# Attention with a gated feed-forward block: sums of a fast matrix product moved between VectorE and GpSimd, and a small attention product moved one block on

## The chip, the cores and the metric

The kernel runs on one core of a Trainium2 chip. A core has engines that run side by side, each through its own instructions in order: TensorE (PE in the profile, its weight loads PEld) multiplies matrices into PSUM; VectorE (DVE) and ScalarE (ACT) work elementwise on PSUM and SBUF; GpSimd (POOL) works elementwise on SBUF; SyncE (SP) issues most transfers. An instruction that needs another engine's result waits for a semaphore, and everything behind it on its engine waits too. The metric is the device time of one execution in microseconds; less is better.

## The reference

Inputs are q, k and v with 8 batches, 8 heads, 576 positions and 64 features, and three weight matrices. For each batch and head:

```python
q_s = softmax(q, axis=-1)          # over the 64 features
k_s = softmax(k, axis=2)           # over the 576 positions
kv  = einsum('bhsd,bhse->bhde', k_s, v)
x   = einsum('bhsd,bhde->bhse', q_s, kv)
# x as 4608 rows of 512 features
out = (gelu(x @ w_gate) * (x @ w_val)) @ w_out     # 512 -> 1536 -> 512
```

The result is 4608 rows of 512, in float32.

## The kernel before, in words

**Blocks.** The rows are done in nine blocks of 512. Block b below 8 has positions of batch b; block 8 gathers the 64 positions that each of the 8 batches has left over. The order is 0 to 6, 8, 7. While the feed-forward of a block runs, the attention for later blocks is prepared beside it: exp of q and k on ACT, q's normalisation (`norm_pair`: a sum and a reciprocal on DVE, two multiplies on POOL), a transpose of q by a transfer (`unit_td`, L385), casts of v to half precision on POOL (`cast_v`, L188), kv (`unit_kv4`, L342: 40 small matmuls, then a reciprocal and a multiply on DVE) and x (`unit_x4`, L429).

**The feed-forward from block 3 on.** The hidden features, 1536, are twelve tiles of 128, called ht 0 to 11. Some tiles are made plainly: `half` makes "7g" (gate of tile 7, 4 matmuls of 512 columns, then Gelu on ACT) and "7v" (value, then the product on DVE, L626). The others are made in pairs k and k+3 by a fast scheme for two by two matrices that needs seven products in place of eight (`pair_step`). It needs sums of x (`sum_x`, L592, four subtractions on POOL) and of the weights (`sum_wgv`, L586, on DVE). A pair has four steps, written k.1 to k.4. Step 1 does products 1 and 5 and copies on ACT (L659 and `snap`, L639), step 2 products 6 and 3 and an addition on DVE (L643), step 3 products 7 and 2, another addition (L643), the first `final` (L632, L633) and `upper` (Gelu on ACT, L647, then a multiply, L649, on POOL, but on DVE for pair 8), step 4 product 4 and the second `final`. Product 4 adds into the bank that step 3's addition reads, so it waits for that addition.

**The output product.** `out_strassen` multiplies ht by w_out in the same scheme, product 1 to 7 (L711) in the banks psa, psb and psc. It copies a bank (`snap`, L743), adds (L749) into yo, and stores. It needs four sums of h (`sum_h`, L575): 1 and 2 go to separate tiles; 3 is written over a part of ht; 4 into s4. Each handles two j of six at a time. For j of 0 and 3, and of 1 and 4, they are made early, during the steps (names s0 and s1): 1 and 2 on DVE, 3 and 4 on POOL. For j of 2 and 5, which come last, all four are made within `out_strassen` on DVE. Product 5 needs sum 1, product 6 sum 2, product 3 sum 4, product 7 sum 3.

**The order.** It is written out by hand, and each engine runs its instructions in the order in which the program issues them. For blocks 3 to 8 the strings THREE, FOUR and SIX list the steps; letters are hooks: "a" and "n" the two halves of `norm_pair` for the next block, "t" the transpose of its q, "l" loads, "s0" and "s1" sums of h. Functions are hung on hooks with `at(block, kind, name, ...)` and run by `ride`. Kind PR means a name of these strings or "e" (exp of q and k, in `out_strassen`); kind NS means a place within `out_strassen`: 1 to 4 after products 5, 6, 3 and 7. Weight sums hang on NS 1 to 3, v's casts on NS 2, x, kv and the sums of x on NS 4. There is one buffer for exp of k and one for v in half precision, so exp of k and casts of v for a later batch must follow kv of the one before.

**Banks.** PSUM has 8 banks in a free list, `ring`; a new tile takes the oldest free one and waits for that bank's last reader.

Of the kernel before, what the change touches and what calls it, by code (L numbers as in the profile page):

```python
# [18 lines left out]
def kernel(  # L19
# [12 lines left out]
    B, H, S, D = q.shape  # L32
# [16 lines left out]
    NO = NFI // 2  # L49
# [43 lines left out]
    def let_go(t):  # L93
        ring.append(held.pop(id(t))[1])
# [26 lines left out]
    for i, nm in enumerate("gv"):  # L121
        n = 3 * NO * P
# [4 lines left out]
    xs_b = [xs, ld_b["v"][0].rearrange("p h x -> p (h x)").bitcast(f16)[:, 0:2048].rearrange(  # L127
        "p (i c r) -> p i c r", i=4, c=2)]
# [271 lines left out]
    def get_xt(b):  # L400
        if (b, "xt") not in st:
            st[(b, "xt")] = att.tile([P, HP, MAIN], f16, name="xt", tag="xt")
        return st[(b, "xt")]
# [161 lines left out]
    def sum_h(j0, j1, which, eng="dve"):  # L565
        step = 1 if j1 - j0 == 2 else NO // 2
        js, ks = slice(j0, j1, step), slice(NO + j0, NO + j1, step)
        a11, a21 = ht[:, js, 0:256], ht[:, js, 256:512]
        a12, a22 = ht[:, ks, 0:256], ht[:, ks, 256:512]
        s1, s2 = sh[1][:, js], sh[2][:, js]  # L570
        for i in which:
            o, a, b, op = {1: (s1, a21, a22, ALU.add), 2: (s2, s1, a11, ALU.subtract),
                           3: (a21, a11, a21, ALU.subtract),
                           4: (s4[:, js], a12, s2, ALU.subtract)}[i]
            (nc.gpsimd if eng == "pool" else nc.vector).tensor_tensor(out=o, in0=a, in1=b, op=op)  # L575
# [12 lines left out]
    def sum_x(xt, xs=xs):  # L588
        b11, b12, b21, b22 = (xt[:, c:c + 2, r:r + 256] for c in (0, 2) for r in (0, 256))
        t = [xs[:, i] for i in range(4)]  # L590
        for o, a, b in ((t[0], b12, b11), (t[1], b22, t[0]), (t[2], b22, b12), (t[3], b21, t[1])):
            nc.gpsimd.tensor_tensor(out=o, in0=a, in1=b, op=ALU.subtract)  # L592

    def product_gv(i, ps, xt, k, first):
# [3 lines left out]
        for t, w, nm in ((0, wv_sb, "v"), (1, wg_sb, "g")):  # L598
            ss = ws[(nm, k // NO)]
            for c in range(2):  # L600
# [6 lines left out]

    THREE = ("a 6g l 6v n 0.1 9g 0.2 9v t 0.3 7g 0.4 s0 1.1 7v 1.2 10g 1.3 10v 1.4 s1 2.1 8g 2.2"  # L610
             " 8v 2.3 11g 2.4 11v")
    FOUR = ("a 7g l 7v n 0.1 6.1 0.2 6.2 t 0.3 6.3 10g 0.4 6.4 s0 1.1 10v 1.2 8g 1.3 8v 1.4 s1 2.1"
            " 11g 2.2 11v 2.3")
    SIX = ("0.1 6.1 0.2 6.2 0.3 6.3 0.4 1.1 6.4 s0 7.1 1.2 7.2 1.3 7.3 1.4 2.1 7.4 s1 8.1 2.2 8.2"
           " 2.3 8.3 2.4")
    steps = {b: (THREE if b == 3 else SIX if b >= B - 1 else FOUR).split() for b in range(3, B + 1)}
    live = {}

# [82 lines left out]
    def product(i, ps, first, ts=(0, 1), js=range(NO)):  # L701
        for j in js:
            for t in ts:
                c0, c1 = slice(t * P, (t + 1) * P), slice(256 + t * P, 256 + (t + 1) * P)
                a = {1: ht[:, j, c0], 2: ht[:, NO + j, c0], 3: s4[:, j, c0], 4: ht[:, NO + j, c1],
                     5: sh[1][:, j, c0], 6: sh[2][:, j, c0], 7: ht[:, j, c1]}[i]
                w = {1: wo_sb[:, j, 0:256], 2: wo_sb[:, NO + j, 0:256],
                     3: wo_sb[:, NO + j, 256:512]}.get(i)
                if w is None:
                    w = tw[{4: 4, 5: 1, 6: 2, 7: 3}[i]][:, j]  # L710
                nc.tensor.matmul(ps[t], a, w, start=(first and j == js[0] and (  # L711
                    t == ts[0] or ps[t].tensor is not ps[ts[0]].tensor)),
                                 stop=(j == js[-1]), skip_group_check=True)

    def get_x(b):
        return get_xt(b) if b < B else xtr

    def last_js(b):
        return (NO - 2 if b < 3 else NO // 2 - 1, NO)

    def out_strassen(b, last):
        yo = [yop.tile([P, 2, C], f32, name="yo", tag="yo") for _ in range(2)]
        c = (slice(0, 256), slice(256, 512))
        ps, tiles_ = {}, {}

        def get(nm):
            if last:
                tiles_[nm] = [big([P, 256], f32, "ps" + nm, True) for _ in range(2)]
                ps[nm] = [x for x in tiles_[nm]]
            else:  # L730
                tiles_[nm] = [big([P, 2, 256], f32, "ps" + nm, True)]
                ps[nm] = [tiles_[nm][0][:, t] for t in range(2)]

        def parts(nm):
            return [(0, ps[nm][0]), (1, ps[nm][1])] if last else [(slice(0, 2), tiles_[nm][0])]

        def snap(nm):
            sn = ffn.tile([P, 2, 256], f32, name="sn", tag="gl")
            for n, (t, src) in enumerate(parts(nm)):
                if n:  # L740
                    nc.scalar.activation(out=sn[:, t], in_=src, func=ACTF.Copy, scale=1.0 / _H_SCALE)
                else:
                    nc.vector.tensor_scalar(out=sn[:, t], in0=src, scalar1=1.0 / _H_SCALE,  # L743
                                            scalar2=None, op0=ALU.mult)
            return sn

        def add(nm, sn, half, col):
            for t, src in parts(nm):
                nc.vector.scalar_tensor_tensor(  # L749
                    out=yo[half][:, t, c[col]], in0=src, scalar=1.0 / _H_SCALE,  # L750
                    in1=sn[:, t], op0=ALU.mult, op1=ALU.add)

        js = (0, 1, 2, 3, 4, 5) if b < 3 else (0, 3, 1, 4, 2, 5)
        get("a")
        product(1, ps["a"], True, js=js[:4])
        if b > 3:
            pair_step(b, get_x(b), NO // 2 - 1 if b < B - 1 else NFI - NO // 2 - 1, 4)
        ride(b, PR, "e")
        get("b")
        if 3 < b < B - 1:  # L760
            product(2, ps["b"], True, js=js)
        product(1, ps["a"], False, js=js[4:])
        sum_h(*last_js(b), (1, 2))
        s1 = snap("a")
        if not 3 < b < B - 1:
            product(2, ps["b"], True, js=js)
        add("b", s1, 0, 0)
        for x in tiles_["b"]:
            let_go(x)
        sum_h(*last_js(b), (4,))  # L770
        get("c")
        product(5, ps["c"], True, js=js)
        sum_h(*last_js(b), (3,))
        s5 = snap("c")
        ride(b, NS, 1)
        product(6, ps["a"], False, js=js)
        s2 = snap("a")
        ride(b, NS, 2)
        product(3, ps["c"], False, js=js)
        add("c", s2, 0, 1)  # L780
        ride(b, NS, 3)
        for x in tiles_["c"]:
            let_go(x)
        store_rows(b, 0, yo[0])
        if last:
            finish_last(b, ps["a"], yo[1], s5)
            return
        product(7, ps["a"], False, js=js)
        add("a", s5, 1, 1)
        ride(b, NS, 4)  # L790
        if b == B:
            go_on(B - 1, get_x(B - 1), 1)
        product(4, ps["a"], False, js=js)
        nc.scalar.activation(out=yo[1][:, :, c[0]], in_=tiles_["a"][0], func=ACTF.Copy,
                             scale=1.0 / _H_SCALE)
        let_go(tiles_["a"][0])
        store_rows(b, 1, yo[1])
# [97 lines left out]
    FI, NS, PR = range(3)  # L895
    plan = {}

    def at(b, kind, i, *fns):
        plan.setdefault((b, kind, i), []).extend(fns)

    L = lambda f, *a: (lambda: f(*a))
# [46 lines left out]
    for b in range(3, B):  # L948
        n = b + 1
# [12 lines left out]
    for b in range(2, B - 1):  # L962
        n = b + 1
        at(b, NS, 4, L(unit_x4, n, ("act", "dve"), 0 if n == B - 1 else None))
        if n + 1 < B:
            at(b, NS, 4, L(unit_kv4, n + 1, True))
        if b == 2:
            at(b, NS, 4, L(sum_wgv, "v", 4), L(sum_wgv, "v", 3), one_ring)
        if b < 6:
            at(b, NS, 4, L(preload, ACTF.Gelu))  # L970
        at(b, NS, 4, L(lambda n: sum_x(get_x(n)), n if n < B - 1 else B))
    at(B, PR, "s0", L(lambda: sum_x(get_x(B - 1), xs_b[1])))
    for b in range(3, B + 1):
        for j in range(NO // 2 - 1):
            at(b, PR, f"s{j}", L(sum_h, j, NO, (1, 2)), L(sum_h, j, NO, (3, 4), "pool"))
    for b, i, what in ((3, 1, "g1 v1"), (3, 2, "g2 v2 g3 v3"), (3, 3, "g4 v4")):
        for x in what.split():
            at(b, NS, i, L(sum_wgv, x[0], int(x[1]), NO, 1))
# [6 lines left out]
    def ride(b, kind, i):  # L985
        for fn in plan.get((b, kind, i), []):
            fn()
# [63 lines left out]
```

## Time and profile before

The median of three runs is 302.79 us (302.77 to 302.89). The profiled execution took 302.76 us, and its span from the first to the last instruction is 300.9 us.

| what | value |
|---|---|
| busy, share of the span | PE 285.8 us (95%), DVE 224.8 (75%), ACT 187.9 (62%), POOL 172.0 (57%) |
| granted TensorE clock | 1.00 |
| block 3, from its first matmul to block 4's | 113.86 to 144.84 us |
| blocks 4, 5, 6 | 144.84 to 176.07, to 207.30, to 237.13 |
| block 8 | 237.13 to 268.16 |
| block 7 and the end | 268.16 to 300.90 |
| a sum of h | DVE 417 to 526 ns, POOL 1154 and 1376 |
| a sum of x on POOL | 1154 to 1239 ns |
| a norm multiply on POOL | 1290 ns |

A line of the timeline gives start, duration, engine, source line, operation, the tiles written and read, and in brackets how long the engine stood idle before it and who released it. A line of the waits gives the total, the number and the longest. DMA engines are busy 56% of block 3 and 6% of block 8.

### The profile page before, as it was taken

Reading aid. Unit: us, or ns where it says so; the run is one execution under the profiler, and the core shown is the slowest. Engines: PE = TensorE matmul, PEld = TensorE weight load, DVE = VectorE, ACT = ScalarE, POOL = GpSimd, SP = SyncE. Lnnn points to the kernel's source line nnn. Section 1 sums busy time; section 2 is a strip of 40 time slices with the busy share of each in tenths; the row PEclk is TensorE's granted clock in tenths of the full one; section 3 lists DMA queues with packets and bytes.
Section 4 is the critical chain, followed back from the end, with each engine's and each line's share of the span. In section 5 each row is a group of like instructions: output and inputs, shape, how many; then the busy total and the mean of one; then the engine's idle time right before and its main releaser. Section 6 shows DMA issues by size and latency. Waiting matters only on the chain. (4 is left out here: it accounts for less than half of the span.)

```text
span 300.9 us, 6202 instructions
## 1 busy us (share of the span) xinstructions
PE 285.8 (95%) x2401; PEld 198.8 (66%) x2401; DVE 224.8 (75%) x430; ACT 187.9 (62%) x305; POOL 172.0 (57%) x157
## 2 busy tenths in 40 slices
PE   3999999999999999999999899989999998899994
PEld 1544445447744586668777777777768786788884
DVE  2943478998677889769876996889678586946792
ACT  4763467767652566676866877686861677338740
POOL 1557557870346009873896579757972579504720
PEclk9999999999999999999999999999999999999999
DMA  7999999996189106930697049603130300033003
GB/s 230 372 383 390 401 388 395 324 309 179 74 291 314 26 34 226 369 73 2 191 379 150 1 163 382 156 0 137 37 67 0 142 2 2 0 72 70 2 1 142
DMA packets 54622, 51.72 MB, mean 172 GB/s; under 512 B 18496, under 2 KB 50496, under 8 KB 54592
## 3 DMA queue, kind: packets, MB, share of 16 engines
q1 hardware_dynamic: 52864, 49.49, 51.9%
q10 hardware_dynamic: 1728, 1.84, 1.9%
q8 instruction: 19, 0.31, 0.4%
q14 instruction: 11, 0.09, 0.1%
HBM read 37.75 MB, written 9.44 MB: 157 GB/s over the span
## 5 line engine op out<-in xcount | busy, mean ns | idle before, releaser
L466 PE MATMUL psg<-xt,wg_sb 128*128 128x512 f16 x216 | 57.4, 379 | 0.0
L466 PE MATMUL psv<-xt,wv_sb 128*128 128x512 f16 x216 | 57.4, 379 | 0.0
L249 POOL TENSOR_TENSOR eq<-eq,rrq 128x640 f16<-128x640 f16 (+1 forms) x27 | 34.7, 1304 | 19.5 <-DVE rrq L242 7.2
L711 PEld LDWEIGHTS <-ht 128*128 128x128 f16 x384 | 37.2, 98 | 6.0 <-issue 0.8
L471 ACT ACTIVATE gl<-psg 128x512 f32<-128x512 f32 x36 | 21.0, 598 | 28.8 <-PE psg L466 28.6
L472 DVE SCALAR_TENSOR_TENSOR ht<-psv,gl 128x512 f16<-128x512 f32 x36 | 24.2, 684 | 16.0 <-PE psv L466 13.7
L466 PEld LDWEIGHTS <-wv_sb 128*128 128x128 f16 x216 | 21.1, 98 | 22.3 <-issue 0.2
L466 PEld LDWEIGHTS <-wg_sb 128*128 128x128 f16 x216 | 21.0, 98 | 20.7
L605 PEld LDWEIGHTS <-wv_sb 128*128 128x128 f16 x216 | 20.9, 98 | 11.3 <-issue 3.0
L649 POOL TENSOR_TENSOR ht<-eq 128x512 f16<-128x512 f32 x13 | 16.5, 1272 | 20.5 <-ACT eq L647 20.5
L188 POOL CAST v<-vt 128x640 f16<-128x640 f32 x26 | 20.2, 818 | 12.0 <-PE pskv L342 10.5
L592 POOL TENSOR_TENSOR xs<-xt 128x512 f16<-128x512 f16 x8 | 9.6, 1194 | 29.3 <-ACT xt L190 29.3
L711 PE MATMUL psa<-tw,ht 128*128 128x256 f16 x192 | 23.5, 273 | 0.1
L605 PEld LDWEIGHTS <-wg_sb 128*128 128x128 f16 x216 | 21.1, 98 | 2.5
L212 ACT ACTIVATE ek<-kt 128x1280 f16<-128x1280 f32 (+1 forms) x11 | 19.1, 1748 | 5.7 <-DMA kt<-in_k_dram 4.2
L659 ACT COPY pgb<-pga 128x512 f32<-128x512 f32 x27 | 15.9, 590 | 10.2 <-PE pga L605 10.0
L633 DVE SCALAR_TENSOR_TENSOR ht<-pga,glq 128x256 f16<-128x256 f32 x27 | 11.1, 422 | 13.7 <-ACT glq L632 13.7
L711 PEld LDWEIGHTS <-sh 128*128 128x128 f16 x192 | 18.8, 98 | 3.7 <-issue 1.6
L575 POOL TENSOR_TENSOR ht<-ht 128x512 f16<-128x512 f16 x12 | 16.5, 1376 | 6.3 <-DVE sh L575 6.3
L632 ACT ACTIVATE glq<-pgb 128x256 f32<-128x256 f32 x27 | 10.2, 378 | 15.8 <-PE pgb L605 9.5
L212 ACT ACTIVATE eq<-qt 128x2560 f16<-128x2560 f32 (+2 forms) x10 | 18.4, 1863 | 2.6 <-DMA qt<-in_q_dram 2.5
L605 PE MATMUL pga<-xs,wv_sb 128*128 128x256 f16 x84 | 16.0, 272 | 2.9 <-DVE eq L643 2.3
(161 smaller groups left out, 677.8 us busy)
## 6 DMA issues: line engine op xcount, KB each, us to landing
out_dram<-yo SPq DMA_DIRECT2D x15, 512.0 KB, 3.4
kt<-in_k_dram SPq DMA_DIRECT2D x7, 640.0 KB, 8.9
vt<-in_v_dram SPq DMA_DIRECT2D x7, 640.0 KB, 5.4
qt<-in_q_dram SPq DMA_DIRECT2D x7, 640.0 KB, 7.3
qt<-in_q_dram SPq DMA_DIRECT2D x8, 512.0 KB, 7.7
wost<-in_moe_w_out_dram SPq DMA_DIRECT2D x6, 512.0 KB, 7.9
kt<-in_k_dram SPq DMA_DIRECT2D x6, 512.0 KB, 9.7
vt<-in_v_dram SPq DMA_DIRECT2D x6, 512.0 KB, 6.0
```

The costliest lines, as they stand in the source:

```text
L188: nc.gpsimd.tensor_copy(out=dst, in_=src)
L212: nc.scalar.activation(out=dst[:, n0:NC, h0 * D:h1 * D].rearrange(o, d=D, **({"t": 2} if b >= QUAD else {})), in_=heads(tiles[(nm, b)], b, ...
L249: (nc.gpsimd if eng == "pool" else nc.vector).tensor_tensor(out=e, in0=e, in1=rrq.unsqueeze(-1).to_broadcast((P, n, 2, D)), op=ALU.mult)
L466: nc.tensor.matmul(ps, w[:, ci, fi * P:(fi + 1) * P], xt[:, ci, :], start=(ci == 0), stop=(ci == HP - 1))
L471: nc.scalar.activation(out=gl, in_=psg, func=ACTF.Gelu)
L472: nc.vector.scalar_tensor_tensor(out=ht[:, fi, :], in0=psv, scalar=_H_SCALE, in1=gl, op0=ALU.mult, op1=ALU.mult)
L575: (nc.gpsimd if eng == "pool" else nc.vector).tensor_tensor(out=o, in0=a, in1=b, op=op)
L605: nc.tensor.matmul(ps[:, t], a, x, start=(first and t == 0 and c == 0), stop=(c == 1), skip_group_check=True)
L633: nc.vector.scalar_tensor_tensor(out=ht[:, fi, 0:256], in0=ps[:, 0], scalar=_H_SCALE, in1=gl, op0=ALU.mult, op1=ALU.mult)
L649: (nc.vector if k == NFI - NO // 2 - 1 else nc.gpsimd).tensor_tensor(out=ht[:, k:k + NO // 2 + 1:NO // 2, 256:512], in0=cc[:, :, 0], in1=c ...
L659: nc.scalar.copy(out=pb, in_=pa)
L711: nc.tensor.matmul(ps[t], a, w, start=(first and j == js[0] and (t == ts[0] or ps[t].tensor is not ps[ts[0]].tensor)), stop=(j == js[-1]), ...
```

## The change

It changes the order of work and, for some sums, the engine; the arithmetic is the same.

- In `out_strassen`, sums 4 and 3 of the last j go to POOL for blocks above 2; both are issued ahead of v's casts at NS 2.
- A new place NS 0 lies after the first eight matmuls of product 1. kv of batches 5, 6 and 7 moves there, from NS 4 of blocks 3, 4, 5 to NS 0 of blocks 4, 5, 6. kv of batch 4 stays in block 2.
- Sums of x for block 7 move from s0 of block 8 to NS 4 of block 6, behind those for block 8.
- The hooks s0 and s1 keep sums 1 and 3; sums 2 and 4 go to new hooks u0 and u1. In the strings, sums stand later: in THREE both behind 7v, in FOUR behind 1.1, 1.2, 2.1 and 2.2, in SIX behind 7.1, 1.3, 8.1 and 2.3.
- In THREE, "n" moves behind 0.4, 1.1 ahead of 7v, and "t" behind 1.1.

```diff
-    THREE = ("a 6g l 6v n 0.1 9g 0.2 9v t 0.3 7g 0.4 s0 1.1 7v 1.2 10g 1.3 10v 1.4 s1 2.1 8g 2.2"
-             " 8v 2.3 11g 2.4 11v")
-    FOUR = ("a 7g l 7v n 0.1 6.1 0.2 6.2 t 0.3 6.3 10g 0.4 6.4 s0 1.1 10v 1.2 8g 1.3 8v 1.4 s1 2.1"
-            " 11g 2.2 11v 2.3")
-    SIX = ("0.1 6.1 0.2 6.2 0.3 6.3 0.4 1.1 6.4 s0 7.1 1.2 7.2 1.3 7.3 1.4 2.1 7.4 s1 8.1 2.2 8.2"
-           " 2.3 8.3 2.4")
+    THREE = ("a 6g l 6v 0.1 9g 0.2 9v 0.3 7g 0.4 n 1.1 t 7v s0 u0 1.2 10g 1.3 10v 1.4 s1 u1 2.1 8g"
+             " 2.2 8v 2.3 11g 2.4 11v")
+    FOUR = ("a 7g l 7v n 0.1 6.1 0.2 6.2 t 0.3 6.3 10g 0.4 6.4 1.1 s0 10v 1.2 u0 8g 1.3 8v 1.4 2.1"
+            " s1 11g 2.2 u1 11v 2.3")
+    SIX = ("0.1 6.1 0.2 6.2 0.3 6.3 0.4 1.1 6.4 7.1 s0 1.2 7.2 1.3 u0 7.3 1.4 2.1 7.4 8.1 s1 2.2"
+           " 8.2 2.3 u1 8.3 2.4")
...
         product(1, ps["a"], True, js=js[:4])
+        ride(b, NS, 0)
         if b > 3:
...
-        sum_h(*last_js(b), (4,))
+        sum_h(*last_js(b), (4,), "pool" if b > 2 else "dve")
         get("c")
         product(5, ps["c"], True, js=js)
-        sum_h(*last_js(b), (3,))
+        sum_h(*last_js(b), (3,), "pool" if b > 2 else "dve")
...
     for b in range(2, B - 1):
         n = b + 1
         at(b, NS, 4, L(unit_x4, n, ("act", "dve"), 0 if n == B - 1 else None))
-        if n + 1 < B:
+        if b == 2:
             at(b, NS, 4, L(unit_kv4, n + 1, True))
+        if b > 3:
+            at(b, NS, 0, L(unit_kv4, n, True))
...
-    at(B, PR, "s0", L(lambda: sum_x(get_x(B - 1), xs_b[1])))
+    at(6, NS, 4, L(lambda: sum_x(get_x(B - 1), xs_b[1])))
     for b in range(3, B + 1):
         for j in range(NO // 2 - 1):
-            at(b, PR, f"s{j}", L(sum_h, j, NO, (1, 2)), L(sum_h, j, NO, (3, 4), "pool"))
+            at(b, PR, f"s{j}", L(sum_h, j, NO, (1,)), L(sum_h, j, NO, (3,), "pool"))
+            at(b, PR, f"u{j}", L(sum_h, j, NO, (2,)), L(sum_h, j, NO, (4,), "pool"))
```

## The prediction

> **What bounds the kernel now.** I read the page first: busy shares, then the chain that ended last, then the waits of PE, then the timelines around each wait.
>
> ```profile
> PE 285.8 (95%) x2401; PEld 198.8 (66%) x2401; DVE 224.8 (75%) x430; ACT 187.9 (62%) x305; POOL 172.0 (57%) x157
> ...
> PE 11%; DVE 1%; issue 0%
> ```
>
> PE is busy 95% of the 300.9 us span and carries the chain, so an edit counts only where PE stands still. PE's waits from 113 us on, where all edits lie:
>
> ```profile
> PE pga L605 <- DVE eq L643: 2.3, 2, 1.2
> PE psc L711 <- DVE sn L743: 1.5, 3, 0.5
> PE psa L711 <- DVE sn L743: 1.2, 2, 0.6
> PE pga L605 <- DVE cc L643: 0.6, 1, 0.6
> ```
>
> All are PE waiting for DVE. PE's timeline places them (the wait in brackets):
>
> ```profile
> 121.58 0.39 PE L605 MATMUL pga<-xs,wv_sb 128*128 128x256 f16 x2 [0.62 <-DVE cc L643]
> ...
> 168.67 1.47 PE L711 MATMUL psa<-tw,sh 128*128 128x256 f16 x12 [0.61 <-DVE sn L743]
> 170.67 1.47 PE L711 MATMUL psc<-wo_sb,s 128*128 128x256 f16 x12 [0.52 <-DVE sn L743]
> ...
> 250.35 0.38 PE L605 MATMUL pga<-xs,wv_sb 128*128 128x256 f16 x2 [1.17 <-DVE eq L643]
> ```
>
> Recorded ends carry pipeline latency, so I measure gaps by starts (12 matmuls of 256 columns take 1.31, 4 of 512 take 0.87): block 3: 0.78; blocks 4 and 5: 0.77+0.69 each; block 6: 0.59; block 8: 1.34, 1.30, 0.30. Together 7.2 us, the most that can be won. Why DVE is late, from DVE's and POOL's timelines in block 8:
>
> ```profile
> 246.10 1.11 DVE L575 TENSOR_TENSOR sh<-ht 128x512 f16<-128x512 f16 x1
> 247.24 1.26 DVE L575 TENSOR_TENSOR sh<-sh,ht 128x512 f16<-128x512 f16 x1
> 248.43 0.68 DVE L643 SCALAR_TENSOR_TENSOR eq<-pgc,snq 128x512 f32<-128x512 f32 x1
> ...
> 245.78 1.15 POOL L592 TENSOR_TENSOR vt<-xt 128x512 f16<-128x512 f16 x1
> 247.00 1.22 POOL L592 TENSOR_TENSOR vt<-xt,vt 128x512 f16<-128x512 f16 x1
> ```
>
> A sum of h takes DVE 0.42 alone; here each ends 0.28 after a POOL instruction ends (246.93, 248.22). The sums at 166.26 and 167.20 lie so against v's casts (0.91, 0.82).
>
> **The skill.** The Trainium skill's "SBUF — State Buffer", section "Who interferes with whom", gives DVE and GpSimd one shared port pair with an exclusive lock; its section "SBUF: two separate sides" says the lock is held for a whole instruction and counts DVE instructions with two SBUF inputs. The lines above agree; additions with one PSUM input keep 0.68 beside POOL. "Perfetto Trace Analysis", section "GPSIMD Instruction", advises timing POOL by start-to-start spacing: I use 1.12 for a sum of h or x (recorded 1.15; 1.40 behind a DVE sum), 1.22 for a norm multiply, 1.23 for upper's multiply (L649), 0.66 for a cast of v.
>
> **The change, part by part.** Times are before's own, unless called new.
>
> *Block 3: norm's second half behind step 0.4, sums 1 and 2 of h together behind 7v.* Removed: DVE's reduce (1.47) and reciprocal no longer stand before the additions of step 0.3, so its addition ends at about 120.5, step 0.4 starts unhindered at 120.80 and 1.1 follows. Added: after 0.4's last DVE instruction (new 122.05 to 122.5) come the reduce to 123.9, the reciprocal to 124.2, and 7v's product to 124.75. POOL's two norm multiplies run from 124.2 to 126.7. Sum 1 wants to start at 124.7, waits for the first multiply (125.5) and ends at 125.78; sum 2 waits for the second and ends at 126.98. Behind them on DVE: the addition of 1.2 to 127.6 and that of 1.3 to 128.2. Step 1.4 overwrites what the latter reads and starts at 128.25, where 127.24 was before and 126.45 was free: **+1.0**, the 0.78 won included. Without the lock it would be 126.98, or -0.26.
>
> The transpose of eq (one DMA on SP) leaves at about 126.75 instead of 122.88. Landing 6.4 to 8.4 later, it is done by 135.2; the next exp of q, which overwrites eq, starts at 135.43 plus this shift, and SP's next job is the store at 141.75. Cost nothing; uncovered, ACT would slip, with 2.4 us of idle before 142.44.
>
> *kv one block on.* Its 40 matmuls (0.75 on PE) leave blocks 3, 4, 5 and enter 4, 5, 6: PE's work is unchanged. Exp of k now waits for kv, but stands behind a table load and the exp of q (3.6 us) on ACT: nothing. Kv's reciprocal and multiply (0.17+0.42) fall into DVE's 0.83 idle before step 2.4's product: nothing. Following the free list by hand, kv takes 8v's bank, long read. But kv had covered something: between x's matmuls and product 4, which overwrites psa after yo's addition has read it. That addition ends 0.9 after product 7; x's matmuls cover 0.7. Any lateness of DVE there now reaches PE.
>
> *Third and fourth sums of the last pair on POOL ahead of the casts.* DVE loses 2 times 0.33. Sums 1 and 2 no longer meet the casts: in block 4 they end at new 167.5 (upper on POOL being 0.3 later, since sum 2 of s1 moved), the copy of psa at 168.2, before product 6 wants it at 168.66. POOL makes sum 4 to 168.7 and sum 3 to 169.85; product 3 wants the fourth at 169.97, product 7 the third at 171.28. So 0.77+0.69 is won in blocks 4 and 5, and 0.59 in 6. But casts now run from 169.8 to 172.9, onto DVE's weight sums (L586, 0.42 each). In block 4: g1 ends 171.45, g2 172.3, yo's addition 172.9, g4 173.2, next yo's addition 173.86; product 4 starts at 173.9 instead of 174.75: **-0.85**. Block 5 (two sums, norm of the rest 0.9): 205.6 against 205.98: **-0.38**. Block 6 (no casts, kv added): 236.0 against 235.82: **+0.18**. Block 3: eight small sums among the casts, product 4 at 144.53 against 143.51: it keeps its **+1.0**.
>
> *Sums of x of block 7 with block 8's, and single sums, block 8.* POOL's eight sums run to 245.65, so upper of pairs 0 and 6 ends at 248.1 (245.8 before). Sum 1 waits for it, runs clear to 248.57; then additions, 1.3's to 250.36: step 1.4 at 250.41 against 250.35. That stall stays: the lock is exchanged for a queue. Sum 2 behind 1.3 pushes ACT's copies by 0.37, so 2.2 and 8.2 start 0.2 to 0.4 later. Upper of 7 ends at 254.7, sum 1 at 255.2, addition of 2.3 at 257.28: step 2.4 at 257.33 against 258.09. Call that addition's end A. POOL's upper of pair 2 ends at A+2.02, with its fourth sum queued behind it (u1 comes after 2.3). DVE's own upper of pair 8 (two SBUF inputs; alone about 0.69 by "VectorE: DVE Perf Modes", section "The TRN2 errata — SBUF-src ops pay a fixed extra latency per instruction") is ready at A+2.0. A tie. If POOL is first, DVE ends at A+3.7, the product of 8.4 and psb's last two matmuls wait, and product 3 starts at 264.24 against 264.50: **-0.26**. If DVE is first: 263.69, -0.81. In the first case the shorter copy chain behind psc also takes away the 0.30.
>
> *Single sums in blocks 4 to 6.* Sum 1 of s0 waits for upper as before (155.81); sum 2, now behind 1.2's addition, meets POOL's sum 3 and ends at new 157.71; 1.3's addition ends at 158.33 (158.49 before) and step 1.4 starts at 158.97. Of s1 it fills 0.3 of the idle time that was 0.76, and 2.3's addition ends at 164.5, before 2.4 at new 165.16, which kv pushed back. Nothing; without kv there, 0.1.
>
> *Block 7.* No wait of PE to win here. Sum 2 behind 1.3 and 2.3 moves additions and ACT's copies by 0.31 and PE with them. The same tie: POOL first, psb waits 0.8 more and product 3 starts at 294.12 against 293.02: **+1.1**; DVE first: +0.32.
>
> **Sum.** POOL first: 1.0-0.85-0.38+0.18-0.26+1.1 = +0.8. DVE first: 1.0-0.85-0.38+0.18-0.81+0.32 = -0.54. The profiled execution took 302.76, 1.86 outside its span, and the median is 302.79: 303.6, or 302.25. I take POOL first, because its instruction waits ready in the queue while DVE's still needs ACT's result.
>
> **Rivals.** (1) DVE gets the pair first, in both blocks: 302.25, not slower. It decides at A+2.0: a gelu 0.05 earlier suffices. For it: at 135.28 a DVE sum asking 0.1 before a cast ended was let in ahead of the next. Against: no such margin here. (2) Block 3's sums pass the norm multiplies: 1.25 us less, 302.3 with POOL first, 301.0 with DVE first. For it: multiplies of the norm starting 0.5 sooner or sums 2 us later would do. Against: all three starts hang on one reciprocal, and the DVE subtraction from 61.47 to 63.37 (1.9, the one before it 0.96) waited out just such a multiply, which ended at 62.55. (3) The simple reading: all named stalls go and nothing comes, 7.2 us less, 295.6. Against: 1.9 us of POOL queue in block 8 and the lost cover behind x. I give it next to nothing. (4) More goes late than I found, such as a slipped exp on ACT or casts meeting every weight sum: block 4 and 5 win nothing (+1.2 on the sum): 304.8.
>
> **Numbers.** POOL first 0.40, DVE first 0.26, block 3 clear 0.12, more late 0.20, all stalls gone 0.02. About 0.2% (0.6 us) is what can be told from no change. Faster (below 302.2): half of DVE first, most of block 3 clear: 0.22. Within: the other half, and the lower end of POOL first: 0.30. Slower (above 303.4): 0.48. Both signs hold most of the chance; POOL first alone spans 303.0 to 304.2. The range, 301.5 to 304.8, reaches from block 3 clear to more late.
>
> **What would show it.** Right: no wait at 168.67 and 170.67 and their likes; step 1.4 of block 3 waiting nearly 2 us for an addition, with two sums of h over 1 us on DVE; product 4 of blocks 3 to 5 waiting for yo; 1.4 of block 8 still waiting over 1 us; psb of block 7 waiting for ht behind a long L649 on DVE. Wrong: sums of 0.42 in block 3, POOL's eight sums of x not delaying upper, or L649 on DVE below 0.8 in blocks 8 and 7.

## The result, and the profile after

The changed kernel takes 302.95 us (median; 302.83 to 303.24) beside 302.78 us for the kernel before in the same session (302.76 to 302.89). The ratio is 1.0006, with a 95% interval of 0.9989 to 1.0023: no change that can be told. One run below was profiled in an execution of 309.05 us at a granted clock of 0.95, so of it only the time of its three other executions is used.

The page of the changed kernel, busy times and the chain that ended last:

```profile
PE 285.7 (95%) x2401; PEld 198.5 (66%) x2401; DVE 220.8 (73%) x418; ACT 188.2 (63%) x305; POOL 184.3 (61%) x169
...
PE 7%; ACT 2%; DVE 1%; issue 1%; ACTq 0%
```

DVE has lost 4.0 us of work and POOL has gained 12.3, as meant; PE's busy time and the span (301.0 against 300.9 us) have not moved. PE's waits from 113 us on, after the change (total, number, longest); yo is written by the additions of the output product, sn by the copies of its banks, and eq and cc at L643 by the additions of a pair:

```profile
PE pga L605 <- DVE eq L643: 3.2, 2, 1.8
PE psa L711 <- DVE yo L749: 2.2, 3, 0.9
PE pga L605 <- ACT pgb L659: 0.3, 2, 0.2
```

The 2.7 us for the copies sn are gone, and so is the wait for cc. In their place stand 2.2 us for yo and 0.9 more for eq. PE's timeline says where:

```profile
128.45 0.38 PE L605 MATMUL pga<-xs,wv_sb 128*128 128x256 f16 x2 [1.81 <-DVE eq L643]
144.83 1.47 PE L711 MATMUL psa<-tw,ht 128*128 128x256 f16 x12 [0.80 <-DVE yo L749]
175.24 1.47 PE L711 MATMUL psa<-tw,ht 128*128 128x256 f16 x12 [0.46 <-DVE yo L749]
206.10 1.47 PE L711 MATMUL psa<-tw,ht 128*128 128x256 f16 x12 [0.92 <-DVE yo L749]
250.91 0.38 PE L605 MATMUL pga<-xs,wv_sb 128*128 128x256 f16 x2 [1.35 <-DVE eq L643]
```

These are waits of the same kind, PE for DVE, and all but the last stand at new places: step 1.4 of block 3, product 4 of blocks 3, 4 and 5, step 1.4 of block 8. To see what each block won or lost, take one fixed point in each, the start of product 4 in blocks 3 to 6 and of product 3 in 8 and 7; "block" is the time from the point before to this one. The two runs at the right are described below.

| start of | before | after | block, before | block, after | only the last pair's sums moved | all but kv moved |
|---|---|---|---|---|---|---|
| block 2, product 4 | 112.54 | 112.57 | | | 112.65 (start) | 112.75 (start) |
| block 3, product 4 | 143.51 | 144.83 | 30.97 | 32.26 | 31.10 | 32.25 |
| block 4, product 4 | 174.75 | 175.24 | 31.24 | 30.41 | 29.76 | 29.99 |
| block 5, product 4 | 205.98 | 206.10 | 31.23 | 30.86 | 29.82 | 30.12 |
| block 6, product 4 | 235.82 | 236.21 | 29.84 | 30.11 | 29.25 | 29.46 |
| block 8, product 3 | 264.50 | 264.31 | 28.68 | 28.10 | 28.38 | 28.11 |
| block 7, product 3 | 293.02 | 293.16 | 28.52 | 28.85 | 28.52 | 28.85 |

So the change won 0.83 + 0.37 + 0.58 us in blocks 4, 5 and 8 and lost 1.29 + 0.27 + 0.33 in blocks 3, 6 and 7. In block 3, DVE's timeline shows the two sums that the prediction expected beside the norm's multiplies:

```profile
124.63 1.16 DVE L575 TENSOR_TENSOR sh<-ht 128x512 f16<-128x512 f16 x1
125.83 1.37 DVE L575 TENSOR_TENSOR sh<-sh,ht 128x512 f16<-128x512 f16 x1
```

They take 2.53 us where two of 0.42 would do. And the tie of block 8, first DVE's lines and then POOL's:

```profile
259.83 0.69 DVE L649 TENSOR_TENSOR ht<-cc 128x512 f16<-128x512 f32 x1
...
260.77 1.04 DVE L575 TENSOR_TENSOR sh<-ht 128x512 f16<-128x512 f16 x1
```

```profile
259.85 1.69 POOL L575 TENSOR_TENSOR s<-ht,sh 128x512 f16<-128x512 f16 x1
```

DVE's multiply started 0.02 us ahead of POOL's sum, took its clear 0.69, and POOL's sum of 1.15 recorded 1.69; DVE's next sum, beside it, took 1.04 in place of 0.42. Block 7 shows the same: DVE at 289.01, POOL at 289.03. That is the opposite of what the prediction chose.

### The profile page after: what moved, and what is told of

Its sections match the earlier page's. It is cut to its first block, busy times and chain, and to the rows that moved or that the text cites. A ratio compares the mean times of both kernels' runs of the same rounds, so it can differ in the third digit from the quotient of the medians.

```text
span 301.0 us, 6201 instructions
## 1 busy us (share of the span) xinstructions
PE 285.7 (95%) x2401; PEld 198.5 (66%) x2401; DVE 220.8 (73%) x418; ACT 188.2 (63%) x305; POOL 184.3 (61%) x169
## 5 line engine op out<-in xcount | busy, mean ns | idle before, releaser
L575 POOL TENSOR_TENSOR s<-ht,sh 128x512 f16<-128x512 f16 x18 | 21.9, 1215 | 10.8 <-DVE sh L575 10.8
L649 POOL TENSOR_TENSOR ht<-eq 128x512 f16<-128x512 f32 x13 | 16.5, 1272 | 17.0 <-ACT eq L647 17.0
L575 POOL TENSOR_TENSOR ht<-ht 128x512 f16<-128x512 f16 x18 | 21.2, 1179 | 6.1 <-DVE sh L575 6.1
```

The lines of the kernel that those rows point to most:

```text
L649: (nc.vector if k == NFI - NO // 2 - 1 else nc.gpsimd).tensor_tensor(out=ht[:, k:k + NO // 2 + 1:NO // 2, 256:512], in0=cc[:, :, 0], in1=c ...
```

## Experiments

The theory is that of the prediction: PE waits only where DVE is late, and DVE is late because its sums with two SBUF inputs wait while POOL works, or because POOL's queue brings their input late. What is open is which part of the change pays and which costs. The diffs show the orders and calls that differ, shortened. Unless said otherwise each run is the changed kernel with one edit. Times are medians; the kernel before took 302.78 to 302.92 in these sessions.

### Sums of block 3 behind step 1.3

```diff
-1.1 t 7v s0 u0 1.2 10g 1.3 10v 1.4
+1.1 t 7v 1.2 10g 1.3 s0 u0 10v 1.4
```

> The changed kernel with one edit: in block 3 both sums of h of the first pair stand behind step 1.3 in place of step 1.2, so the additions of 1.2 and 1.3 no longer queue behind them on DVE while POOL multiplies the norm. Theory (sums held up by POOL's norm multiplies through the shared port pair, additions queued behind them): step 1.4 of block 3 starts at about 126.5 in place of 128.45, nothing comes back later in the block, time 302.95 - 1.9 = 301.0 us. Rival (the wait is only the reduce and reciprocal of the norm on DVE, or the slack is eaten at 2.4 by sums that now meet sums 3 and 4 on POOL): 1.4 or 2.4 still waits over 1 us, time 302.5 to 303.0.

Measured: 301.95 us, 0.9969 of before (0.9957 to 0.9981). The wait at 1.4 is gone, but DVE's second sum of the first pair now meets POOL's multiply of upper, that of the next pair meets POOL's fourth sum, and step 2.4 waits. DVE's timeline, POOL's, then PE's:

```profile
127.19 1.38 DVE L575 TENSOR_TENSOR sh<-sh,ht 128x512 f16<-128x512 f16 x1
...
129.90 1.26 DVE L575 TENSOR_TENSOR sh<-sh,ht 128x512 f16<-128x512 f16 x1
```

```profile
126.97 1.31 POOL L649 TENSOR_TENSOR ht<-eq 128x512 f16<-128x512 f32 x1
...
129.54 1.33 POOL L575 TENSOR_TENSOR s<-ht,sh 128x512 f16<-128x512 f16 x1
```

```profile
133.00 0.38 PE L605 MATMUL pga<-xs,wv_sb 128*128 128x256 f16 x2 [0.60 <-DVE cc L643]
```

Step 1.4 had lost 1.97 us, measured by starts. Half of it is won (product 4 of block 3 comes 1.0 us sooner), half is given back one pair later: between the two expectations.

### The norm's multiplies behind the sums

```diff
-0.4 n 1.1 t 7v s0 u0 1.2
+0.4 n 1.1 7v s0 u0 m t 1.2      # n: reduce and reciprocal; m: the two multiplies on POOL
```

> The changed kernel with one edit: in block 3 the two POOL multiplies of the norm's second half, and the transpose issue, stand behind the sums of s0 and u0 in the order, the norm's reduce on DVE stays where it is. Theory (DVE's two sums of h take 1.16 and 1.37 us because POOL's multiplies work beside them): the sums take about 0.42 each, step 1.4's wait of 1.81 us falls to under 0.4. But POOL's product of the upper half of pair 1 now waits behind the multiplies until about 131, so the sums of s1 come late and step 2.4 waits some 1.5 us instead: 302.6 to 302.9. Rival (the reduce itself, 1.2 us of DVE ahead of the sums, is what is late): the sums take 0.4 but step 1.4 still waits over 1 us, and the time is 303.5 or more.

Measured: 303.14 us, 1.0010 (1.0002 to 1.0019). DVE's sums, then PE's next wait:

```profile
124.58 0.41 DVE L576 TENSOR_TENSOR sh<-ht 128x512 f16<-128x512 f16 x1
125.03 0.42 DVE L576 TENSOR_TENSOR sh<-sh,ht 128x512 f16<-128x512 f16 x1
```

```profile
134.03 0.38 PE L606 MATMUL pga<-xs,wv_sb 128*128 128x256 f16 x2 [1.51 <-DVE cc L644]
```

The reduce stands where it stood, at 122.33 and 1.48 long, and the sums take 0.41 and 0.42. So the 1.7 us of block 3 are the multiplies beside the sums, and the rival, the reduce, falls. The time is not won, because the upper product of pair 1 now queues behind the multiplies (it starts at 130.00), and step 2.4 waits 1.51, as expected. The total came 0.24 above the expected range.

### kv at its old place

```diff
-at(b, NS, 0, L(unit_kv4, n, True))       # b = 4, 5, 6
+at(b, NS, 4, L(unit_kv4, n + 1, True))   # b = 3, 4, 5
```

> The changed kernel with kv back at its old place, between x and product 4 (blocks 3, 4, 5), the rest as changed. Theory (kv covered the wait of product 4 for yo's addition; at its new place it covers nothing, so its 0.75 us on PE comes on top): block 3 ends as in the changed kernel, blocks 4 and 5 end 0.3 earlier each, block 6 loses the 0.75 and wins about 0.5; waits of PE for yo shrink to 0.2 or less; time about 301.9 us. Rival A (kv's place makes no difference, since PE's work is the same): 302.8 to 303.1. Rival B (all three waits for yo, 2.2 us, come from the move): 300.8.

Measured: 301.16 us, 0.9945 (0.9931 to 0.9960), faster than both kernels. All of PE's waits from 113 us on:

```profile
PE pga L605 <- DVE eq L643: 3.2, 2, 1.8
PE pga L605 <- ACT pgb L659: 0.3, 2, 0.2
```

No wait for yo is left. The ledger's last column differs from the changed kernel by 0.42, 0.74 and 0.65 us in blocks 4, 5 and 6: kv's move alone costs 1.8 us. Kv's 40 matmuls take 0.75 us wherever they stand; standing ahead of product 4 they fill time that PE would wait, and standing in product 1 they fill none. In block 3 product 4 starts at the same distance with kv and without (32.25 and 32.26); of three times 0.75 us, 1.81 is so filled. The expectation of 1.05 was too small.

### Sums of x of block 7 back in block 8

```diff
-at(6, NS, 4, L(lambda: sum_x(get_x(B - 1), xs_b[1])))
+at(B, PR, "s0", L(lambda: sum_x(get_x(B - 1), xs_b[1])))
```

> The changed kernel with the sums of x of block 7 back at the first sums of h of block 8, the rest as changed. Theory (the stall at step 1.4 of block 8 was only changed from a lock into a queue behind eight sums of x on POOL): POOL's two uppers end 2 us earlier, 1.4 waits less than 0.3 in place of 1.35, but POOL is late for pair 7 and step 2.4 waits about 1.3; block 8 is about 0.5 shorter, time 302.4 us. Rival (moving them was worth what it seems to be, a stall less): time 303.6 or more, with both stalls over 1 us.

Measured: 303.12 us, 1.0008 (0.9998 to 1.0018). DVE's second sum, and PE's waits of 0.5 us and more in block 8:

```profile
250.21 1.35 DVE L575 TENSOR_TENSOR sh<-sh,ht 128x512 f16<-128x512 f16 x1
```

```profile
252.22 0.38 PE L605 MATMUL pga<-xs,wv_sb 128*128 128x256 f16 x2 [0.73 <-DVE cc L643]
...
258.45 0.38 PE L605 MATMUL pga<-xs,wv_sb 128*128 128x256 f16 x2 [0.56 <-DVE eq L643]
```

One wait of 1.35 turns into one of 0.73 and one of 0.56. Beside the other parts, this part of the change is neutral: POOL's sums of x cost about as much ahead of its products as beside DVE's sums.

### The last pair's sums back on DVE

```diff
-sum_h(*last_js(b), (4,), "pool" if b > 2 else "dve")      # and so for (3,)
+sum_h(*last_js(b), (4,))
```

> The changed kernel with the last pair's third and fourth sums of h back on DVE in all blocks, the rest as changed. Theory (on POOL they keep the casts away from sums 1 and 2 and take 0.66 from DVE ahead of psc's copy, at the price of casts falling on the weight sums): waits of product 6 and product 3 come back in blocks 4, 5 and 6 at 0.3 to 0.6 each, block 3 wins 0.5 because its eight weight sums run clear, blocks 4 and 5 lose 0.7 each, blocks 6 and 8 lose 0.3 to 0.5; time about 304.5 us. Rival (the two ways of meeting POOL are worth the same): 302.8 to 303.2.

Measured: 305.22 us, 1.0081 (1.0064 to 1.0098), so undoing this part costs 2.3 us. Two of PE's waits in this run:

```profile
PE psc L711 <- DVE sn L743: 2.2, 5, 0.6
PE psa L711 <- DVE yo L749: 0.6, 3, 0.2
```

Psc waits for its copy again. But the wait for yo shrank from 2.2 us to 0.6, so an estimate of what these sums are worth by themselves is 2.3 + 1.6 = 3.9.

### The last pair's sums alone

The kernel before, with that one edit.

> The kernel before with one part of the change alone: the last pair's third and fourth sums of h on POOL, all else as before. Theory (the psc snapshot waits for DVE behind these sums; putting them back on DVE in the changed kernel cost 2.3 us, and kv at its old place covers the waits for yo): 300.7 to 301.3. Rival (without the other parts POOL has not finished its casts and upper products by then, and products 3 wait for the fourth sum): 302.5 to 303.5.

Measured: 299.17 us, 0.9879 (0.9864 to 0.9894): 3.7 us faster than before, 1.5 below the expected range, which had been read off the run above without the wait that it hid. PE's waits from 113 us on, then sums 1 and 2 of block 4 on DVE, before and in this run, and POOL in this run:

```profile
PE pga L605 <- DVE eq L643: 2.3, 2, 1.2
PE pga L605 <- DVE cc L643: 0.6, 1, 0.6
```

```profile
166.26 0.91 DVE L575 TENSOR_TENSOR sh<-ht 128x512 f16<-128x512 f16 x1 [0.37 <-POOL ht L649]
167.20 0.82 DVE L575 TENSOR_TENSOR sh<-sh,ht 128x512 f16<-128x512 f16 x1
```

```profile
166.47 0.43 DVE L575 TENSOR_TENSOR sh<-ht 128x512 f16<-128x512 f16 x1 [0.37 <-POOL ht L649]
166.93 0.42 DVE L575 TENSOR_TENSOR sh<-sh,ht 128x512 f16<-128x512 f16 x1
167.28 0.68 DVE L743 TENSOR_SCALAR sn<-psa 128x512 f32<-128x512 f32 x1
```

```profile
167.44 1.16 POOL L575 TENSOR_TENSOR s<-ht,sh 128x512 f16<-128x512 f16 x1 [1.00 <-DVE sh L575]
```

Sums 1 and 2 took 0.91 and 0.82 before, beside v's casts. POOL now has sum 4 queued ahead of the casts, and sum 4 needs sum 2, so POOL stands still while DVE makes its two: 0.43 and 0.42. The copy of psa stands right behind these two. The copy of psc stood behind sums 4 and 3 as well, two of 0.42 that are now gone from DVE. In block 6 no casts run and sums 1 and 2 took 0.43 and 0.42 before too, so there only the second effect is at work. Both waits of psc and psa for sn are gone, and with kv still in front of product 4 none for yo takes their place. By the ledger this one edit wins 1.48, 1.41, 0.59 and 0.30 us in blocks 4, 5, 6 and 8. All the rest of the change gives it back: 1.16 in block 3, 0.23, 0.30 and 0.21 in blocks 4 to 6 by the order of the sums, 1.81 by kv, 0.33 in block 7, less 0.28 in block 8.

### The norm's second half earlier (kv at its old place)

```diff
-a 6g l 6v 0.1 9g 0.2 9v 0.3 7g 0.4 n 1.1 t 7v s0 u0 1.2 10g 1.3 10v 1.4 s1 u1 2.1 8g 2.2 8v 2.3 11g 2.4 11v
+a 6g l 6v 0.1 9g 0.2 9v 0.3 n 7g 0.4 1.1 t 7v s0 1.2 10g 1.3 u0 10v 1.4 2.1 8g s1 2.2 8v 2.3 u1 11g 2.4 11v
```

> The changed kernel with kv at its old place (measured alone: 301.16) and block 3's order rewritten: norm's second half stands ahead of half 7g, where DVE shows about 1 us of idle time, and the sums u0 and s1 stand one step later each. Theory (the stall of 1.97 us at step 1.4 of block 3 comes from the norm beside the sums): it falls to under 0.5, and 299.6 to 300.0 comes out. Rival (the norm's reduce then delays the additions of steps 0.3 and 0.4, and the stall only moves to steps 1.1 to 1.3): 300.8 to 301.3.

Measured: 299.70 us, 0.9897 (0.9880 to 0.9913), as the theory had it. DVE's timeline:

```profile
121.03 1.48 DVE L240 TENSOR_REDUCE rq<-eq 128x20 f32<-128x1280 f16 x1
...
123.85 0.58 DVE L575 TENSOR_TENSOR sh<-ht 128x512 f16<-128x512 f16 x1
...
126.66 0.41 DVE L575 TENSOR_TENSOR sh<-sh,ht 128x512 f16<-128x512 f16 x1
...
128.24 1.36 DVE L575 TENSOR_TENSOR sh<-ht 128x512 f16<-128x512 f16 x1 [0.23 <-POOL ht L649]
```

The reduce moves 1.3 us forward, into time that DVE had idle, and the sums take 0.58 and 0.41. The first sum of the next pair now meets POOL (1.36), but PE does not wait for it: no wait in block 3 is over 0.2 us. Since sums moved too, the 1.46 us against the run with kv alone are those of the whole order.

### Sums of x of block 8 on DVE (kv at its old place)

```diff
+    if mid: mid()          # in unit_x4, behind the copies of xtr: sum_x(xtr) on DVE
```

> The changed kernel with kv at its old place (measured alone: 301.16) and the four sums of x of block 8 on DVE, straight behind the copies of xtr, those of block 7 alone on POOL. Theory (POOL is late in block 8 by the eight sums in a row, and step 1.4's gap of 1.51 us there is POOL's upper product coming late): that gap falls to under 0.4, 299.6 to 300.0. Rival (the sums, some 1.7 us of DVE at the end of block 6, delay DVE's copies of x and the PSUM banks behind them, and a wait of the same length comes at block 8's first steps): 300.9 to 301.5.

Measured: 300.73 us, 0.9931 (0.9915 to 0.9948): 0.4 us under the run with kv alone and 0.2 under the rival's range, far from the theory's. The first mix below, which holds this edit too, shows part of why: the wait of 1.35 at step 1.4 is gone, but one of 0.57 for ACT stands in the first steps of block 8, where the run with kv alone has none. What delays ACT there was not followed.

### Three mixes

All three have kv at its old place, the early norm, the order of before in blocks 4 to 6 and the edit just named. The first keeps the changed order in blocks 7 and 8, the second takes the order of before there (s0 and u0 together ahead of 7.1), the third sets them together behind 7.1.

> A version put together from the parts that paid: kv at its old place; the last pair's sums on POOL; block 3's order with the norm early (as in the run that measured 299.70); blocks 4 to 6 with the order of before, so that sums of h of one step stand together; blocks 7 and 8 with the order of the changed kernel; sums of x of block 8 on DVE behind the copies of xtr, those of block 7 on POOL ahead of block 8. From the start points of the runs so far: 299.70, less 0.75 for blocks 4 to 6, less 0.7 to 1.4 for block 8, so 297.5 to 298.3. Rival (DVE's sums of x at the end of block 6 only move the wait of block 8, as the 0.33 us gained by that run suggests): 298.6 to 299.2.

> As the mix before it in this call, with the order of before in blocks 7 and 8 too (the sums s0 and u0 ahead of step 7.1, s1 and u1 ahead of 8.1). Theory (the two gaps of 1.35 and 1.30 us that this order showed in block 8 come from POOL being late with its eight sums of x, not from where DVE's sums stand): both gaps under 0.4, and 297.0 to 298.0. Rival (the order itself: DVE's two sums wait at the head of its queue for POOL's upper product): one of the gaps stays at 0.7 us or more, 298.3 to 299.0.

> As the first mix of this call, with s0 and u0 together, and s1 and u1 together, behind steps 7.1 and 8.1 in blocks 7 and 8, where DVE showed about 1 us of idle time ahead of steps 1.2 and 2.2. Theory: the four sums fall into idle time, POOL's fourth sum is over before the last product of the upper half, and 297.0 to 297.8 comes out, 0.3 us under the first mix. Rival (the second sum ahead of step 1.2's additions makes them late by its 0.42 us): 0.3 us over the first mix or more.

Measured: 298.31 us (0.9852; 0.9837 to 0.9867), 297.35 us (0.9818; 0.9804 to 0.9833) and 297.32 us (0.9818; 0.9802 to 0.9834). The second's waits of PE:

```profile
PE pga L607 <- ACT pgb L661: 0.6, 1, 0.6
PE psa L713 <- DVE sn L745: 0.2, 1, 0.2
```

Both gaps of block 8 are gone in all three, and the second has the order that showed them, so they came from POOL being late with its sums of x, of which it now makes four in place of eight. What is left of PE's waits there is the 0.57 in the first steps. Pairing the sums is worth 1.0 us against splitting them (298.31 to 297.35): from product 4 of block 6 to product 3 of block 8 it takes 27.61 us split and 26.93 paired, and to that of block 7 28.85 and 28.52. One reason is in the traces of block 8: split, POOL's fourth sum meets DVE's multiply of pair 8 again (1.69 and 0.69, and 1.04 for DVE's next sum); paired, it is over by then, and multiply and sum take 0.80 and 0.41. Whether the pair stands ahead of 7.1 or behind makes no difference. In blocks 4 to 6 the order of before gives 29.78, 29.82 and 29.25 us; with the split sums, in the run with the early norm, it was 30.00, 30.14 and 29.46. This second mix beats the kernel before by 5.6 us.

### DVE's multiply of pair 8 a little later

```diff
+    nc.scalar.copy(out=late_t, in_=cc[:, 1, 0, 0:112])     # ahead of upper's Gelu, pair 8 only
```

> The changed kernel with one copy of 128x112 on ACT, into a tile that nobody reads, between the addition of step 8.3 and the Gelu of the upper half of pair 8 (blocks 8 and 7 alone). It makes DVE's multiply of pair 8 ready some 0.1 to 0.2 us later, where it had beaten POOL's fourth sum by 0.02 us in both blocks. Theory (the two take turns, and the one that starts first decides, as the prediction's tie has it): POOL's sum now runs first in 1.15 us, DVE's multiply records 1.5 us or more in place of 0.69, psb's last matmuls wait for ht, product 3 of block 8 comes some 0.55 later and that of block 7 some 0.8 later: 304.0 to 304.4. Rival (who is first does not matter, or DVE goes first anyway): 0.1 to 0.4 us for the later Gelu alone, 303.0 to 303.4, with the multiply still at 0.7 to 0.8.

Measured: 308.21 us, 1.0178 (1.0161 to 1.0195), outside both ranges; the profile separates two things. Blocks 0 and 1 already end 3.96 us later (product 4 of block 1 starts at 84.32 against 80.36), where the edit does nothing but lay one more tile of 448 bytes per partition into SBUF (see the last section). From there to product 4 of block 6 the two agree (240.17 - 236.21 = 3.96). In block 8, DVE's line, POOL's and PE's:

```profile
263.92 1.59 DVE L652 TENSOR_TENSOR ht<-cc 128x512 f16<-128x512 f32 x1 [0.22 <-ACT cc L650]
```

```profile
263.81 1.16 POOL L576 TENSOR_TENSOR s<-ht,sh 128x512 f16<-128x512 f16 x1
```

```profile
265.91 0.39 PE L714 MATMUL psb<-wo_sb,ht 128*128 128x256 f16 x2 [0.65 <-DVE ht L634]
```

POOL starts 0.11 ahead, its sum takes the clear 1.16, and DVE's multiply 1.59 in place of 0.69. Product 3 comes 0.48 later in block 8 and 0.83 more in block 7 (expected 0.55 and 0.8). So the tie is worth 1.3 us in all, and it turned when the Gelu ahead of DVE's multiply started 0.14 us later.

## Why the prediction was right or wrong

**Right by its range, wrong in its case.** 302.95 lies in 301.5 to 304.8 and in "no change", which had 0.30; the likeliest case, POOL first at 303.6, did not come. That the time came so close to before's is in part luck: the case that came had been put at 302.25, and mis-sized terms make up the difference.

**The step that failed** is the tie in blocks 8 and 7: "I take POOL first, because its instruction waits ready in the queue while DVE's still needs ACT's result." POOL's instruction stood in the queue, but behind POOL's own multiply, and DVE's started 0.02 us ahead of it: L649 on DVE took 0.69 in both blocks, below the 0.8 that the prediction had named as a sign against it. The late multiply shows that the step had the mechanism and the prices right: 0.48 + 0.83 = 1.31 us between the two cases, where the prediction had 0.55 + 0.78 = 1.33. Only the choice was wrong, in both blocks.

**DVE first was given -0.54**, and the profile shows +0.14 at product 3 of block 7. The difference of 0.68 is mis-sized terms: block 3 was +1.29 and not +1.0 (0.29), block 8 -0.58 and not -0.81 (0.23), block 6 +0.27 and not +0.18 (0.09), and 0.07 in the start and the other blocks. In block 3, 0.2 of it is the second sum, which ended at 127.20 where 126.98 was forecast, because POOL's two norm multiplies took 2.67 us and not the twice 1.22 used. The 0.23 of block 8 lies in several waits under 0.35 us and was not followed further.

**Blocks 4 and 5** came as worked out: -0.83 and -0.37 where -0.85 and -0.38 stood. The nets hide two large terms, as the prediction named them: the waits for sn won, the cover of kv lost. Where it said "kv had covered something", the runs give the size, 1.81 us over three blocks, against 3.7 us that the last pair's sums are worth.

**Single sums in blocks 4 to 6** were costed at "Nothing; without kv there, 0.1". With kv moved, blocks 4 and 5 came as worked out and leave no room for a cost. With kv at its old place the ledger gives 0.23, 0.30 and 0.21 us, so the 0.1 was two to three times too small.

**Sums of x** went as said: "That stall stays: the lock is exchanged for a queue." Step 1.4 of block 8 waits 1.35 where it waited 1.17, and undoing the move changes the time by 0.17 us (303.12 against 302.95).

**The lock.** The Trainium skill's "SBUF — State Buffer", section "Who interferes with whom", which the prediction leans on, is borne out by the run with the multiplies moved: nothing but POOL's work differs beside DVE's two sums, and they fall from 1.16 and 1.37 us to 0.41 and 0.42. Rival 2, block 3 clear, did not come, since both sums met the multiplies. What a block without that meeting is worth, the prediction put at 0.26 under before; by another order, the run with the early norm brings block 3 to 30.70 us, 0.27 under before. The 0.69 for DVE's multiply, from the Trainium skill's "VectorE: DVE Perf Modes", section "The TRN2 errata — SBUF-src ops pay a fixed extra latency per instruction", is the trace's 0.69.

## What to carry to other kernels

A change of several parts that moves nothing can hold one that is worth 3.7 us and others that give it all back: run each part alone before the whole is dropped. Work of PE that fits into a wait, as kv does ahead of product 4, is worth up to its full length there (1.81 of 2.25 us) and nothing elsewhere, so ask of each moved matmul which wait it was filling. And where DVE's sums of two SBUF inputs meet POOL's work, queue POOL's next instruction so that it depends on DVE's last sum: POOL then stands still while DVE works. The meeting does not vanish, it moves: in the run with the last pair's sums alone, a weight sum of block 4 takes 0.82 in place of 0.42 beside the casts, where PE does not wait for it.

## What the hardware showed that was not expected

- In the pairs of DVE and POOL instructions above, a start 0.02 us ahead was enough: the first ran clear and the second paid most of the first's time. POOL's sum recorded 1.69 in place of 1.15 behind DVE's 0.69; DVE's multiply recorded 1.59 in place of 0.69 behind POOL's 1.16. And the delay is handed back: DVE's next sum, behind POOL's late one, took 1.04 in place of 0.42.
- A scratch tile of 448 bytes per partition, allocated ahead of the other tiles, made the kernel 4 us slower before it did any work of its own. The rate of the loads fell with it: from 20 to 40 us the DMA engines moved 348 and 371 GB/s against 388 and 401, at the same busy share (the view gives 1.09 and 1.07 against 1.09 and 1.06), and PE then waited for weights, which it had not (1.6 us by 90 us). In those stretches the edit changes only where the tiles lie. That the place of the destination sets the rate is argued from this, not shown by a run of its own.
